# Constants from one step matrix, narrow w_in pieces and an earlier flush in a sliding-window attention and MoE kernel

## The chip, the core and the metric

The kernel runs on one core of one Trainium2 chip. The time is device time in microseconds of one execution of the whole program; six runs of the kernel before gave a median of 321.82 us (321.56 to 323.2). The page and the trace describe one further execution, taken by the hardware profiler.

A core has five engines that run their own instruction streams: TensorE (PE, with its weight loads shown apart as PEld), VectorE (DVE), ScalarE (ACT), GpSimd (POOL) and SyncE (SP). POOL and SP issue DMA transfers, which 16 DMA engines of the core carry out. Each stream is executed in its order; streams wait for one another through semaphores.

## What is computed

```python
# q, k, v: [8 batches, 8 heads, 576 positions, 64], float32
mask = np.abs(pos[:, None] - pos[None, :]) <= 32
scores = where(mask, q @ k.T / sqrt(64), -1e9)
x = softmax(scores) @ v                      # as [4608 tokens, 512]
h = x @ w_in                                 # w_in  [512, 2048]
g = where(h >= 1, h, where(h <= -1, 0, (h + 1) ** 2 / 4))
out = g @ w_out                              # w_out [2048, 512], out [4608, 512] float32
```

A query sees only the keys that lie at most 32 positions away, so the scores are a band.

## The kernel before

**Attention.** Keys are taken in blocks of 64. A block of 64 keys meets the 128 queries from 32 before it to 32 behind it, and the band in that tile of 64 x 128 is the same for every block. Two heads lie side by side in the 128 partitions, so partitions 0 to 63 and 64 to 127 hold the same band. `scores` (L201) multiplies keys with queries, takes the exponential on ACT (L225) and applies the band in one of two ways. In the first 14 slots (`eng = None`, L446) the band is added before the exponential: `add_mask` (L194) multiplies the identity with `bias`, 0 inside the band and -1e30 outside, into PSUM. From slot 14 on DVE multiplies the exponentials by `mask4` or `mask8` (L192), which are 1 and 0. `sums` (L255) multiplies the exponentials with v and with ones, and its `end` takes the reciprocal of the row sums on ACT (Ln, L289, then Exp, L290, called lr and rc) and leaves the product of the two for DVE in the list `muls`. `flush` (L301) issues what is in that list: it writes xT, the attention output with tokens along the free axis.

**The second part.** 4608 tokens are cut into 18 blocks of 256 tokens, 2048 hidden columns into 8 pieces of 256. One piece of one block is a slot `a` of the main loop (L444), with t = a // 8 and f = a % 8. In a slot PE computes hp from xT and columns 256 f to 256 f + 256 of w_in (L466, 8 matmuls), ACT makes rr (L470), DVE makes mx and gT (L472, L473). Then `run` issues the attention work that a table of positions (`at`, L366 to L406) gives to this slot, and `quarter` multiplies gT with a quarter of w_out (L417, 4 matmuls) for an earlier block. So slots 0 to 7 need the tokens 0 to 255 and all of w_in, piece by piece; slot 8 needs the tokens 256 to 511, of which the last come from the sums at slots 3, 4 and 5. `quarters` (L363) puts the eight quarters of block 0 at slots 9 to 15; those that use the last quarter of w_out stand at slot 15. A flush stands before hp in slot 0 and in the slots above 5, and one behind gT in every slot.

**The start.** SP loads q of batch 0 as float32. Everything else goes through POOL's queue, which casts to bfloat16 on the way, in this order: k of batch 0, first half (positions come in two halves); v of batch 0; w_in's columns 0 to 512 in four pieces of 256 columns (two halves of the partitions each); q and k of batch 0, second half; the rest of w_in, the columns 512 to 1024 in pieces of 256 and the columns 1024 to 2048 in pieces of 512; w_out's first quarter (L108); q and k of batch 1, first half; w_out's second and third quarters; v of batch 1; w_out's last quarter; q and k of batch 1, second half; batch 2. Loads on POOL's queue take turns on eight semaphores: each waits until the eighth before it has landed. Between k and v POOL makes the identity (`make_identity`), and between v and w_in the four selects that cut the band into `bias` (L127, L129). DVE makes mask4 and mask8 from `bias` by a compare (L343).

**Before the loop** (L327 to L355) q and k of the first half are transposed by PE (`tpose`, L168; with the identity), copied out of PSUM by ACT and DVE in parts (L181), and the first scores and sums are made; `keep_warm` puts in matmuls on zeros. At slots 1 and 1.5 the second half follows: q's transposes, four warm matmuls, k's transposes. The second part of k's transposes uses the PSUM tile that DVE's copy of q's second part has to leave first.

Of the kernel before, what the change touches and what calls it, by code (L numbers as in the profile page):

```python
# [7 lines left out]

FP = mybir.dt.float32
BF = mybir.dt.bfloat16  # L10
AF = mybir.ActivationFunctionType
ALU = mybir.AluOpType
# [3 lines left out]
def kernel(  # L16
# [19 lines left out]
    nc = tc.nc  # L36
    B, H, S, D = q.shape
    NT, DM, DFF = out.shape[0], 512, 2048
# [4 lines left out]
    TAIL = S - MAIN  # L43
# [4 lines left out]
    const = ctx.enter_context(tc.tile_pool(name="const", bufs=1))  # L48
# [13 lines left out]

    ident = const.tile([128, 128], BF, name="ident")
    ones = const.tile([128, 64], BF, name="ones")
    bias = const.tile([128, 128], BF, name="bias")
    mask4 = const.tile([128, 8 * 128], BF, name="mask4")
    mask8 = const.tile([128, 4 * TAIL], BF, name="mask8")
    w_in = const.tile([128, 4, DFF], BF, name="w_in")
# [5 lines left out]
    V, P, A = nc.vector, nc.gpsimd, nc.scalar  # L74
# [20 lines left out]
    def load_v(b, n):  # L95
        if b not in vn:
            vn[b] = nat.tile([128, 2 * NC, 2, D], BF, name="vn", tag="vn", bufs=3)
        h, a = divmod(n, 2)
        y = NY * h + 2 * a
        nc.gpsimd.dma_start(out=vn[b][64 * a:64 * a + 64, :, h], in_=v[b, y:y + 2].rearrange("y s d -> (y s) d")  # L100
                            .rearrange("(c r) d -> r c d", r=64))
# [9 lines left out]
    early = ctx.enter_context(tc.tile_pool(name="early", bufs=1))  # L111
# [5 lines left out]
    A.preload_act_table_set("natural_log_exp_and_others")  # L117
    warm = const.tile([128, 512], BF, name="warm")
    V.memset(warm, 0.0)
    V.memset(bias, 0.0)  # L120
    make_identity(nc, ident)
    for n in range(4):
        load_v(0, n)

    for h in range(2):
        r = slice(64 * h, 64 * h + 64)
        P.affine_select(out=bias[r], in_=bias[r], compare_op=ALU.is_ge, fill=-1e30, base=0,  # L127
                        channel_multiplier=-1, pattern=[[1, 128]])
        P.affine_select(out=bias[r], in_=bias[r], compare_op=ALU.is_ge, fill=-1e30, base=64,  # L129
                        channel_multiplier=1, pattern=[[-1, 128]])  # L130
    V.memset(ones, 1.0)
    for t in qTs:
        V.memset(t[:, 0:PAD], 0.0)
    def mix(small, large):

        for n in range(0, max(len(small), 2 * len(large)), 2):
            for fn, *x in large[n // 2:n // 2 + 1] + small[n:n + 2]:
                fn(*x)

    def halves(b, half):  # L140
        return [(load_long, b, half, t, y) for t in range(2) for y in range(NY)]

    def put(todo):
        for fn, *x in todo:
            fn(*x)

    w = [(load_w_in, c, c + d, h) for c, d in ((0, 256), (256, 256), (512, 256), (768, 256), (1024, 512), (1536, 512))
         for h in range(2)]
    put(w[:4] + halves(0, 1) + w[4:])
    mix(halves(1, 0), [(load_w_out, 0)])  # L150
    put([(load_w_out, 1), (load_w_out, 2)] + [(load_v, 1, n) for n in range(4)])
# [7 lines left out]
    def qkT(b, t):  # L159
        if t == 0:  # L160
            return qTs[b % 3][:, PAD:]
        if b not in kT:
            kT[b] = ktp.tile([128, NY * S], BF, name="kT")
        return kT[b]

    HD = (slice(0, 64), slice(64, 128))
# [27 lines left out]
    def add_mask(ps, n, w):  # L194
        for a in range(2):
            for h in range(2):
                nc.tensor.matmul(ps[h][HD[a], :n * w].rearrange("p (n j) -> p n j", n=n), ident[HD[h], HD[h]],
                                 bias[HD[h], :w].rearrange("p (n j) -> p n j", n=1).to_broadcast([64, n, w]),
                                 start=True, stop=False, skip_group_check=True)

    def scores(b, ys, pars, cs, eng, pool=ps_s):  # L201
# [99 lines left out]
    def flush():  # L301
        while muls:
            muls.pop(0)()
# [4 lines left out]
    def tp1(pool):  # L308
        if pool is ps_h:
            return pool.tile([128, 8, 128], BF, name="tp", tag="hp")  # L310
        return pool.tile([128, 2, 8, 128], BF, name="tp", tag="bb")[:, 0]

    def keep_warm(n, pool, tag):

        z = pool.tile([128, 512], FP, name="z", tag=tag)
        for _ in range(n):
            nc.tensor.matmul(z, warm[:, :128], warm, start=True, stop=True)

    def cast(x, nm, cut):

        y = early.tile([128, 9, 2, D], BF, name=nm)
        o, i = y.rearrange("p j h d -> p h j d"), x.rearrange("p h (j d) -> p h j d", d=D)
        V.tensor_copy(o[:, :, :cut], i[:, :, :cut])
        A.copy(o[:, :, cut:], i[:, :, cut:])
        return y.rearrange("p j h d -> p j (h d)")

    with tc.tile_pool(name="ps_p", bufs=1, space=bass.MemoryType.PSUM) as ps_p:  # L327
        keep_warm(14, ps_h, "hp")

        V.memset(qkT(0, 0).rearrange("d (y s) -> d y s", y=NY)[:, :, S // 2:352], 0.0)  # L330
        for b in range(LONG):
            V.memset(qkT(b, 0).rearrange("d (y s) -> d y s", y=NY)[:, :, S - PAD:], 0.0)
        V.memset(qkT(0, 1).rearrange("d (y s) -> d y s", y=NY)[:, :, S // 2:320], 0.0)
        qn[0, 0] = cast(q32, "qb", 5)
        qq = [tpose(0, n, 0, (A.copy, V.tensor_copy)[n], tp1(ps_h)) for n in range(2)]
        for x in qq:
            x()
        kk = [tpose(0, n, 1, (A.copy, V.tensor_copy)[n], tp1((ps_n, ps_p)[n])) for n in range(2)]
        keep_warm(3, ps_h, "hp")
        for x in kk:  # L340
            x()
        for m, n, w in ((mask4, 8, 128), (mask8, 4, TAIL)):
            V.tensor_scalar(m.rearrange("p (n j) -> p n j", n=n),  # L343
                            bias[:, 0:w].rearrange("p (n j) -> p n j", n=1).to_broadcast([128, n, w]), -1.0, None,
                            op0=ALU.is_ge)
        scores(0, (0, 1), (0, 2), (0, 2), None)
        scores(0, (0, 2), (0, 1), (2, 3), None, ps_n)
        scores(0, (1, 2), (0, 2), (0, 2), None, ps_p)
        keep_warm(5, ps_h, "hp")
        e0 = sums(0, 0, 0, TB)  # L350
        keep_warm(2, ps_h, "hp")
        e1 = sums(0, 1, 0, TB, ps_p)
        keep_warm(8, ps_h, "hp")
        e0()
        e1()  # L355
# [45 lines left out]
    for b in range(LONG, B):  # L401
        a = sl[5 * (b - 1) - 7] - 17
# [22 lines left out]
    def run(pos):  # L425
        todo = []
        for fn, *x in ev.get(pos, []):
            if fn is sums:
                todo.append(sums(*x))
            elif fn is tpose:  # L430
                part = x.pop()
                todo.append(tpose(*x, (A.copy, V.tensor_copy)[part if pos < 2 or pos > 16 else 0], tp1((ps_s, ps_n)[part])))
                if part:
                    while todo:
                        todo.pop(0)()
            elif fn is keep_warm:
                keep_warm(*x)
            else:
                pool = (x.pop(),) if x[-1] in (ps_s, ps_n, ps_o) else ()
                fn(*x, eng, *pool)  # L440
        for end in todo:
            end()

    for a in range(NF * NB + NF):  # L444
        t, f = divmod(a, NF)
        eng = None if a < 14 else V  # L446
        post = [x for n, x in quarters if n == a] if a < 2 * NF else [a - NF]
        for b, x in loads.get(a, []):
            if x < 2:
                load_nat(b, x)  # L450
            else:
                for n in range(4):
                    load_v(b, n)
        if a == 0 or a > 5:
            flush()
        if t < NB:
            if t not in gT:
                gT[t] = gtp.tile([128, 2 * NF, TB], BF, name="gT", tag="gT")
            r0 = TB * t % RING
            if a in (6, 7):  # L460
                hp = ps_o.tile([128, 2, TB], FP, name="hp", tag="op")
            else:
                hp = ps_h.tile([128, 2, TB], FP, name="hp", tag="hp")
            for j in range(2):
                for n, kk in enumerate((0, 2, 1, 3)):
                    nc.tensor.matmul(hp[:, j], w_in[:, kk, 256 * f + 128 * j:256 * f + 128 * j + 128],  # L466
                                     xT[:, kk, r0:r0 + TB], start=n == 0, stop=n == 3)

            rr = ewp.tile([128, 2, TB], FP, name="rr")
            A.activation(rr, hp, AF.Relu, scale=0.5, bias=0.5)  # L470
            mx = ewp.tile([128, 2, TB], FP, name="mx")
            V.tensor_max(mx, hp, rr)  # L472
            V.scalar_tensor_tensor(gT[t][:, 2 * f:2 * f + 2], rr, 1.0, mx, op0=ALU.min, op1=ALU.mult)  # L473
        flush()
        run(a)
        for x in post:
            quarter(x)
        run(a + 0.5)
        for x in xps.get(a, []):
            xpose(*x)  # L480
# [30 lines left out]
```

## Time and profile before

| | |
|---|---|
| median of 6 runs | 321.82 us |
| profiled execution | 322.24 us |
| its span, first to last instruction | 320.4 us |
| granted PE clock over the span | 0.995 |
| PE busy | 306.4 us (96%) |
| DVE busy | 247.3 us (77%) |
| ACT busy | 193.3 us (60%) |
| POOL busy | 87.5 us (27%) |
| DMA packets, bytes | 121573, 34.52 MB |

The span is a little shorter than the time of the execution, which also holds what lies around the first and the last instruction. Busy PE time is not PE at its peak, since matmuls are pipelined and their ends are modelled.

A row of the page's groups gives line, engine, operation and tiles, how often it ran, the busy time, the mean of one in ns, and the idle time of its engine just before with what ended it:

```profile
L466 PE MATMUL hp<-xT,w_in 128*128 128x256 bf16 x1152 | 150.5, 274 | 4.3 <-DMA w_in<-in_moe_w_in_dram 2.7
L417 PE MATMUL op<-w_out,gT 128*128 128x512 bf16 x576 | 146.6, 380 | 0.0
```

The two matmul groups of the second part hold most of PE's time. POOL's timeline of the start gives start, length, engine, line and tiles; the times of the DMA rows are those in which POOL issues them, not those of the transfers:

```profile
3.53 0.25 POOL masks.py:197 MEMSET ident<- 128x128 bf16 x1
3.86 0.29 POOL masks.py:199 TENSOR_SCALAR_AFFINE_SELECT ident<-ident 128x128 bf16<-128x128 bf16 x1
4.10 3.41 POOL L100 DMA_DIRECT2D vn<-in_v_dram  x4
7.47 0.35 POOL L127 TENSOR_SCALAR_AFFINE_SELECT bias<-bias 64x128 bf16<-64x128 bf16 x1
7.89 0.28 POOL L129 TENSOR_SCALAR_AFFINE_SELECT bias<-bias 64x128 bf16<-64x128 bf16 x1
8.24 0.29 POOL L127 TENSOR_SCALAR_AFFINE_SELECT bias<-bias 64x128 bf16<-64x128 bf16 x1
8.60 0.29 POOL L129 TENSOR_SCALAR_AFFINE_SELECT bias<-bias 64x128 bf16<-64x128 bf16 x1
8.84 2.57 POOL L104 DMA_DIRECT2D w_in<-in_moe_w_in_dram  x4
```

### The profile page before, as it was taken

Reading aid. Unit: us, or ns where it says so; the run is one execution under the profiler, and the core shown is the slowest. Engines: PE = TensorE matmul, PEld = TensorE weight load, DVE = VectorE, ACT = ScalarE, POOL = GpSimd, SP = SyncE. Lnnn points to the kernel's source line nnn. Section 1 sums busy time; section 2 is a strip of 40 time slices with the busy share of each in tenths; the row PEclk is TensorE's granted clock in tenths of the full one; section 3 lists DMA queues with packets and bytes.
Section 4 is the critical chain, followed back from the end, with each engine's and each line's share of the span. In section 5 each row is a group of like instructions: output and inputs, shape, how many; then the busy total and the mean of one; then the engine's idle time right before and its main releaser. Section 6 shows DMA issues by size and latency. Waiting matters only on the chain.

```text
span 320.4 us, 8552 instructions
## 1 busy us (share of the span) xinstructions
PE 306.4 (96%) x3651; PEld 202.0 (63%) x3651; DVE 247.3 (77%) x385; ACT 193.3 (60%) x318; POOL 87.5 (27%) x122
## 2 busy tenths in 40 slices
PE   6977899999999999999999999999999999999995
PEld 3555665666666666666666666666666666666652
DVE  2364966797888888888888888888888888877760
ACT  2756656676776666765666666566566766554421
POOL 8982837798204504121411200000000000000000
PEclk9997999999999999999999999999999999999999
DMA  9999999999999999929991947004420000000111
GB/s 144 149 132 202 142 175 159 173 161 165 152 153 172 167 126 176 166 50 104 191 160 41 108 99 117 35 35 106 88 58 35 33 35 35 34 35 35 46 52 65
DMA packets 121573, 34.52 MB, mean 108 GB/s; under 512 B 108736, under 2 KB 116672, under 8 KB 121536
## 3 DMA queue, kind: packets, MB, share of 16 engines
q0 software_dynamic: 92672, 18.06, 72.2%
q1 hardware_dynamic: 28864, 15.93, 21.3%
q8 instruction: 28, 0.46, 0.6%
q14 instruction: 9, 0.07, 0.1%
HBM read 36.70 MB, written 9.44 MB: 144 GB/s over the span
## 4 chain that ended last, share of the span: by engine, by line
PE 83%; POOL 5%; DVE 3%; ACT 3%; DMA 3%; issue 1%; POOLq 0%; ACTq 0%
PE op L417 38%; PE hp L466 37%; PE bb L283 6%; DMA w_in<-in_moe_w_in_dram 3%; PE bb L217 2%; POOL w_in L104 2%; POOL kn L84 1%; PE tp L178 1%; DVE mx L472 1%; POOL vn L100 1%; ACT rr L470 1%; DVE gT L473 1%; POOL qn L84 1%; DVE xT L295 1%; ACT lr L289 1%
## 5 line engine op out<-in xcount | busy, mean ns | idle before, releaser
L466 PE MATMUL hp<-xT,w_in 128*128 128x256 bf16 x1152 | 150.5, 274 | 4.3 <-DMA w_in<-in_moe_w_in_dram 2.7
L417 PE MATMUL op<-w_out,gT 128*128 128x512 bf16 x576 | 146.6, 380 | 0.0
L466 PEld LDWEIGHTS <-w_in 128*128 128x128 bf16 x1152 | 111.9, 98 | 46.2 <-issue 5.4
L470 ACT ACTIVATE rr<-hp 128x512 f32<-128x512 f32 x144 | 85.7, 595 | 91.7 <-PE hp L466 89.5
L472 DVE TENSOR_TENSOR mx<-hp,rr 128x512 f32<-128x512 f32 x144 | 99.3, 690 | 42.0 <-ACT rr L470 40.0
L473 DVE SCALAR_TENSOR_TENSOR gT<-rr,mx 128x512 bf16<-128x512 f32 x144 | 99.6, 692 | 4.9
L417 PEld LDWEIGHTS <-gT 128*128 128x128 bf16 x576 | 53.4, 98 | 41.6
L225 ACT ACTIVATE pt<-bb 128x1024 bf16<-128x1024 f32 (+1 forms) x33 | 33.2, 1012 | 6.3 <-PE bb L217 5.1
L100 POOL DMA_DIRECT2D vn<-in_v_dram x32 | 27.5, 881 | 30.6 <-PE bb L217 29.2
L295 DVE TENSOR_TENSOR xT<-bb,rc 128x512 bf16<-128x512 f32 (+1 forms) x32 | 21.0, 657 | 9.7 <-ACT rc L290 9.1
L422 ACT COPY osb<-op 128x512 f32<-128x512 f32 x36 | 20.8, 581 | 11.6 <-PE op L417 11.2
L290 ACT ACTIVATE rc<-lr 128x512 f32<-128x512 f32 (+2 forms) x40 | 23.5, 587 | 1.3
L92 POOL DMA_DIRECT2D qn<-in_q_dram x10 | 12.3, 1245 | 40.0 <-DMA qT<-qn 40.0
L289 ACT ACTIVATE lr<-bb 128x512 f32<-128x512 f32 (+2 forms) x40 | 22.1, 552 | 1.1 <-PE bb L283 1.0
L283 PE MATMUL bb<-pt,ones 64*64 64x256 bf16 (+3 forms) x352 | 19.7, 258 | 1.3 <-DVE xT L295 0.6
L192 DVE TENSOR_TENSOR pt<-pt,mask 128x1024 bf16<-128x1024 bf16 (+1 forms) x33 | 20.3, 614 | 0.2 <-ACT pt L225 0.2
L283 PE MATMUL bb<-pt,vn 64*64 64x128 bf16 (+3 forms) x712 | 18.5, 206 | 0.0
L283 PEld LDWEIGHTS <-vn 64*64 64x64 bf16 x712 | 17.0, 109 | 0.0
L283 PEld LDWEIGHTS <-ones 64*64 64x64 bf16 x352 | 10.3, 106 | 10.2 <-issue 9.0
L84 POOL DMA_DIRECT2D kn<-in_k_dram x24 | 13.1, 554 | 10.1 <-DMA w_out<-in_moe_w_out_dram 4.3
L217 PE MATMUL bb<-qT,kT 64*64 64x128 bf16 x520 | 13.0, 217 | 0.8 <-DVE kT L181 0.8
L84 POOL DMA_DIRECT2D qn<-in_q_dram x20 | 11.0, 564 | 7.4 <-DMA w_out<-in_moe_w_out_dram 3.1
(44 smaller groups left out, 100.1 us busy)
## 6 DMA issues: line engine op xcount, KB each, us to landing
out_dram<-osb SPq DMA_DIRECT2D x36, 256.0 KB, 2.3
vn<-in_v_dram POOLq DMA_DIRECT2D x32, 144.0 KB, 5.8
qn<-in_q_dram POOLq DMA_DIRECT2D x10, 288.0 KB, 7.3
kn<-in_k_dram POOLq DMA_DIRECT2D x10, 288.0 KB, 8.8
w_out<-in_moe_w_out_dram POOLq DMA_DIRECT2D x4, 512.0 KB, 10.2
kn<-in_k_dram POOLq DMA_DIRECT2D x24, 72.0 KB, 3.9
qn<-in_q_dram POOLq DMA_DIRECT2D x20, 72.0 KB, 4.9
w_in<-in_moe_w_in_dram POOLq DMA_DIRECT2D x8, 128.0 KB, 4.4
```

The source lines that it names most:

```text
L84: (eng or nc.gpsimd).dma_start(out=dst[b, half][32 * y:32 * y + 32], in_=src[b].rearrange("(h y) s d -> y h (s d)", h=2)[y] .rearrange("h ...
L100: nc.gpsimd.dma_start(out=vn[b][64 * a:64 * a + 64, :, h], in_=v[b, y:y + 2].rearrange("y s d -> (y s) d") .rearrange("(c r) d -> r c d", ...
L225: A.activation(p, ps[:, :, :128 * n].rearrange(like, y=m), AF.Exp, scale=D ** -0.5)
L283: nc.tensor.matmul(bb[HD[h], a, o + c0:o + c1], ones[HD[a]] if c is None else vn[b][HD[a], c, h], p(a, h), start=n == 0, stop=True, skip_g ...
L289: A.activation(lr[:, :, :D0], bb[:, :, D0:2 * D0], AF.Ln)
L290: A.activation(rc[:, :, :D0], lr[:, :, :D0], AF.Exp, scale=-1.0)
L295: muls.append(lambda: V.tensor_mul(o, bb[:, :, :D0], rc[:, :, :D0]))
L417: nc.tensor.matmul(o, gT[tt // 2][:, j, 128 * (tt % 2):128 * (tt % 2) + 128], w_out[:, j], start=not done, stop=len(done) == 2 * NF - 1, s ...
L466: nc.tensor.matmul(hp[:, j], w_in[:, kk, 256 * f + 128 * j:256 * f + 128 * j + 128], xT[:, kk, r0:r0 + TB], start=n == 0, stop=n == 3)
L470: A.activation(rr, hp, AF.Relu, scale=0.5, bias=0.5)
L472: V.tensor_max(mx, hp, rr)
L473: V.scalar_tensor_tensor(gT[t][:, 2 * f:2 * f + 2], rr, 1.0, mx, op0=ALU.min, op1=ALU.mult)
```

## The change

Four edits.

- **One step matrix.** A tile `step` of 128 x 257 is set to zero by DVE, and one select on POOL leaves 0 where the column is at least 65 more than the partition, and -1 elsewhere. DVE takes differences of shifted columns of it: by one column for the identity, by 65 for `band` (128 x 192, 1 inside the band and 0 outside); `bias` is (band - 1) times 2 to the 100th. In `band` and `bias` the partitions 64 to 127 have their band 64 columns further right, so users take the columns from 64 h on. The select stands behind k's loads, before v's; the five other POOL instructions go.
- **Masks.** mask4 and mask8 are no longer made by a compare before the loop, but by four copies of `band` (two for each half of the partitions) in slot 1, behind gT and its flush, ahead of the attention work of that slot.
- **w_in** is loaded in pieces of 256 columns throughout: the columns 1024 to 2048 come in eight loads where there were four. The order of the columns stays.
- **Flush.** The flush before hp also stands in the slots 4 and 5.

```diff
-    V.memset(bias, 0.0)
-    make_identity(nc, ident)
+    step = early.tile([128, 257], BF, name="step")
+    V.memset(step, 0.0)
+    P.affine_select(out=step, in_=step, compare_op=ALU.is_ge, fill=-1.0, base=-65, channel_multiplier=-1,
+                    pattern=[[1, 257]])
     for n in range(4):
         load_v(0, n)
-    for h in range(2):
-        r = slice(64 * h, 64 * h + 64)
-        P.affine_select(out=bias[r], in_=bias[r], compare_op=ALU.is_ge, fill=-1e30, base=0,
-                        channel_multiplier=-1, pattern=[[1, 128]])
-        P.affine_select(out=bias[r], in_=bias[r], compare_op=ALU.is_ge, fill=-1e30, base=64,
-                        channel_multiplier=1, pattern=[[-1, 128]])
     V.memset(ones, 1.0)
     for t in qTs:
         V.memset(t[:, 0:PAD], 0.0)
+    V.tensor_sub(ident, step[:, 65:193], step[:, 64:192])
+    V.tensor_sub(band, step[:, 65:], step[:, :192])
+    V.tensor_scalar(bias, band, 1.0, 2.0 ** 100, op0=ALU.subtract, op1=ALU.mult)
...
-    w = [(load_w_in, c, c + d, h) for c, d in ((0, 256), (256, 256), (512, 256), (768, 256), (1024, 512), (1536, 512))
-         for h in range(2)]
+    w = [(load_w_in, c, c + 256, h) for c in range(0, DFF, 256) for h in range(2)]
...
-                                 bias[HD[h], :w].rearrange("p (n j) -> p n j", n=1).to_broadcast([64, n, w]),
+                                 bias[HD[h], 64 * h:64 * h + w].rearrange("p (n j) -> p n j", n=1)
+                                 .to_broadcast([64, n, w]),
...
-        for m, n, w in ((mask4, 8, 128), (mask8, 4, TAIL)):
-            V.tensor_scalar(m.rearrange("p (n j) -> p n j", n=n),
-                            bias[:, 0:w].rearrange("p (n j) -> p n j", n=1).to_broadcast([128, n, w]), -1.0, None,
-                            op0=ALU.is_ge)
...
-        if a == 0 or a > 5:
+        if a == 0 or a > 3:
             flush()
...
         flush()
+        if a == 1:
+            for h in range(2):
+                for m, n, w in ((mask4, 8, 128), (mask8, 4, TAIL)):
+                    V.tensor_copy(m[HD[h]].rearrange("p (n j) -> p n j", n=n), band[HD[h], 64 * h:64 * h + w]
+                                  .rearrange("p (n j) -> p n j", n=1).to_broadcast([64, n, w]))
         run(a)
```

More of the change, by code (lines that the diff above doesn't have):

```diff
@@ L5 @@
 from concourse import mybir
-from concourse.masks import make_identity
 from concourse._compat import with_exitstack
@@ L64 @@
     ones = const.tile([128, 64], BF, name="ones")
-    bias = const.tile([128, 128], BF, name="bias")
+    band = const.tile([128, 192], BF, name="band")
+    bias = const.tile([128, 192], BF, name="bias")
     mask4 = const.tile([128, 8 * 128], BF, name="mask4")
```

## The prediction

> **What bounds the kernel now.** I read the page's slices first. The rows are TensorE (PE), its granted clock, the share of the DMA engines and what they moved, 8 us to a slice:
>
> ```profile
> PE   6977899999999999999999999999999999999995
> ...
> PEclk9997999999999999999999999999999999999999
> DMA  9999999999999999929991947004420000000111
> GB/s 144 149 132 202 142 175 159 173 161 165 152 153 172 167 126 176 166 50 104 191 160 41 108 99 117 35 35 106 88 58 35 33 35 35 34 35 35 46 52 65
> ```
>
> PE is full from slice 5 on, so nothing behind 35 us can be won except where PE waits there. Every part of the change lies in the first five slices, or acts on the loads of the first seven. Next the chain of waits for the start (start, length, what):
>
> ```profile
> 18.94 8.17 DMA w_in<-in_moe_w_in_dram
> 27.11 0.14 issue
> 27.24 1.40 PE hp L466 x8
> ```
>
> The slot loop at a=4 waits for the first w_in piece of 512 columns. Then PE's timeline, with its idle time and the releaser in brackets:
>
> ```profile
> 19.78 0.47 PE L178 MATMUL tp<-ident,kn 128*64 128x128 bf16 x10 [1.01 <-DMA kn<-in_k_dram]
> 20.40 0.41 PE L178 MATMUL tp<-ident,kn 128*64 128x128 bf16 x8 [0.15 <-DVE qT L181]
> ...
> 27.24 1.40 PE L466 MATMUL hp<-xT,w_in 128*128 128x256 bf16 x8 [2.26 <-DMA w_in<-in_moe_w_in_dram]
> ...
> 34.48 1.91 PE L466 MATMUL hp<-xT,w_in 128*128 128x256 bf16 x16 [0.83 <-DVE xT L298]
> ...
> 53.28 0.81 PE L466 MATMUL hp<-xT,w_in 128*128 128x256 bf16 x6 [0.53 <-DVE xT L295]
> ```
>
> Between 34.48 and 53.28 PE has no gap. Last, the windows of the load phase (PE, PEld, DVE, ACT, POOL busy, clock, DMA share, GB/s):
>
> ```profile
> 19.00:22.00 3.00, 1.61 (x25) 1.30 (x26) 2.04 (x3) 0.75 (x1) 3.00 (x6) 1.00 1.13 139
> 22.00:24.00 2.00, 2.00 (x47) 1.35 (x49) 0.99 (x2) 1.66 (x3) 1.21 (x3) 1.00 1.04 132
> 24.00:30.00 6.00, 3.74 (x88) 2.75 (x88) 2.46 (x4) 3.73 (x8) 1.61 (x4) 0.81 1.22 200
> ```
>
> The DMA engines hold work throughout (share about 1 or more). 19 to 22 is 256-column pieces (128 KB over 256 rows, 512 B each), 24 to 30 is 512-column pieces (1 KB rows): 139 against 200 GB/s.
>
> **Part 1, constants (L119 to L133).** Removed on POOL: the identity's memset and select (0.25 + 0.29, with gaps 3.53 to 4.10) and four bias selects (7.51 to 8.89, 1.4 us). Added: one select over 257 columns after the kn loads. 128 columns took 0.29, so 0.29 to 0.6; it ends at about 4.1, where the first vn load started before. So the vn loads keep their time and w_in's first issue moves from 8.84 to about 7.45. That lead mostly turns into queueing: vn's last load lands at 6.63 + 4.2 = 10.9, in the same queue, and the first w_in lands at 12.0 already. DVE gets three small operations (0.2 to 0.3 us each, by the 128x384 compare at 0.28) that wait for the select. Behind them stand five memsets (0.46) and the cast of q at 6.22, which waits for q. 4.1 + 0.8 + 0.5 = 5.4, so 0.8 us of cover; if the select took 1.4 us, every later start would slip. Bias no longer waits on POOL, but L197 at 9.08 also stood behind the three warm matmuls that end there: 0.
>
> **Part 2, masks in slot 1.** The two compares leave 9.01 to 9.62, where DVE then idles 3.84: 0. Two pairs of copies of the same sizes (0.405 and 0.282, 0.61 a pair as overlapped) come after slot 1's gT, which ends at 19.72: 1.15 us in front of the qT copy at 19.64. Behind that copy PE waits (20.40 above), then the kT copy and slot 2. Without the kn wait of 1.01 (kn is issued 1.4 earlier), PE does the first ten kn transposes at 18.8, then idles from about 19.2 to 21.5. Slot 2's hp starts at 21.8 instead of 21.27: this part alone costs 0.5 there.
>
> **Part 3, narrow w_in.** Slot 4 needs only columns 1024 to 1280. POOL issues twelve pieces in the second batch, where eight stood. Landings before (issue plus time to landing): 20.3, 21.1, 21.9, 22.7 for four narrow pieces, 25.8, 27.1, 28.4, 29.7 for four wide ones, w_out's first quarter at 20.74 + 11.6 = 32.3. With 20.0 for the first and 0.9 each, the pairs land at 20.9, 22.7, 24.5, 26.3, 28.1, 29.9. PE, going on from 21.8 with warm durations (hp 0.98 a slot, scores 0.7, 0.46 and sums 0.55), comes to slot 4 at 25.5, slot 5 at 27.0, slot 6 at 28.4, and slot 7 at 29.4: only slot 7 waits, 0.5, and that is covered by the next part.
>
> **Part 4, flush at slots 4 and 5.** The product of slot 3's sums now stands before slot 4's mx. It needs rc, which is in ACT's order ahead of rr, so it runs while ACT makes rr (0.60): 0. Slot 4's product, at 33.35 before because gT of slot 5 was ahead, goes into the DVE idle time ahead of mx. ACT and DVE in their new order (lr 0.55, rc 0.58, rr 0.60; products 0.6, mx and gT 0.69) finish the last product of the first half at 31.65, where it was 34.43. So slot 8 starts at 31.7, not 34.48: **2.8 us earlier** with a warm PE.
>
> The clock takes some of it. After the 2.26 us gap the slice has clock 7, and the 8 matmuls at 29.49 take 1.85 for 1.04. [...] The trace shows half clock after 2.26, from 27.8 to 31.2. The new gap at 19.2 is as long, so by the row hp and scores of slots 2 and 3 run slow: about 1.0 us, and slot 8 at 32.7, 1.8 earlier. Either value stands; the next part makes it matter little.
>
> **Part 5, what is late next: the loads.** Each load waits for the landing of the eighth before it, and the DMA queue is full until 50. w_out's last quarter is issued at 38.00 and lands after 11.6, at 49.6; slot 15's quarter needs it at 50.44. Slack 0.8, and 0.53 more since PE idles before 53.28 anyway: 1.3 us. (qn, kn and the other w_out quarters have 3 us.) The load chain is rigid: the last kn of this group (32.62) waits for w_out's first quarter, the other w_out loads stand behind it, and from there the queue is full. So a shift d of that landing (32.3) moves the landing at 49.6 by d, and the kernel gains at most 1.3 - d.
>
> d from both sides. By landings, 0.79 a piece: 20.0 + 11 x 0.79 + 2.6 = 31.3, d = -1.0. By the rate, 131 KB at 139 GB/s = 0.94: 32.9, d = +0.6; and if the stall between 22.7 and 25.8 (3.1 where a wide piece then takes 1.3) comes again where rows grow at w_out, d = +2.5. [...] I take 0.9, nearer the rate because POOL keeps issuing: 20.0 + 9.9 + 2.6 = 32.5, d = **+0.2**.
>
> **Sum.** Start: -1.8 to -2.8. Given back waiting for w_out at slot 15: 0.7 to 1.7. Net -(1.3 - 0.2) = **-1.1 us**. The profiled execution took 322.24 (span 320.4 and 1.8 around it), so 321.1; on the median of the runs, 321.82, that is **320.7**. A difference under 0.3%, 0.97 us, is about what a measurement here can't tell from none.
>
> **Rivals.**
> - *The loads keep up* (d below -0.5): the start's 1.8 to 2.8 stays, 319.0 to 320.0, say 319.4. For it: landings 0.79 apart, and the 1.4 us lead. Against: the rate. Chance 0.16.
> - *Half clock at slot 15.* PE's wait there is 1 to 2 us; if it halves the clock for 3.4 us, 1.7 us of PE work is lost where PE is the bound: 320.7 + 1.7 = 322.4, no change. For it: the gap at 24.98. Against: 18.8 to 21.3, with 1.6 us of idle in pieces, kept clock 1.00. Chance 0.20.
> - *Slower: narrow rows hold up the loads.* Place: w_out's last quarter in slot 15. From d = 1.3 on it lands too late even for the old schedule. At d = 2 it costs 0.7, and since PE then idles over 2 us in one piece there, half clock adds 1.7: 324.2. For it: 512 B rows at 139 GB/s, 12 x 128 KB of them. Against: it needs the stall again, or 1.02 us a piece. Chance 0.22.
>
> **Numbers.** Forecast (gain 0.5 to 1.9) 0.42; the rivals as given. Faster by over 0.3%: 0.16 and 0.26 of the forecast's 0.42, 0.42. Within: the other 0.16 and 0.15 of half clock, 0.31. Slower: 0.22 and 0.05 of half clock, 0.27. The likeliest's own range is 319.9 to 321.3; for 8 in 10 it reaches to the first rival's 319.4 and well into the slower one, 323.3.
>
> **What would show it.** Right: no PE wait for w_in at slot 4; a wait of 1 to 2.4 us for DVE's qT copy near 21; slot 8 at 31.7 to 32.7; narrow pieces landing 0.8 to 1.0 apart; PE waiting for w_out before the quarters of slot 15 near 49.8. Wrong: no wait there (the loads keep up), the wait in w_in's slots 5 to 7, q's cast later than 6.2, or mask copies much over 1.2 us in sum.

## The result and the profile after

The change makes no difference that this measurement can tell: 321.67 us as the median of 28 runs (320.14 to 323.15) against 321.75 for the kernel before (63 runs), a ratio of 0.9992 with a 95% interval of 0.998 to 1.0003. The forecast was -1.1 us; measured are -0.3 by the ratio and -0.1 by the medians.

The profiled execution after took 322.82 us (span 320.7), so it is one of the long ones; why is seen below. Its slices, in the rows shown of before:

```profile
PE   7969899999999999999999999999999999999995
...
PEclk9987999999999999999999999999999999999999
DMA  9999999999999999929991946005320000000111
GB/s 148 166 141 192 137 177 163 179 159 168 150 148 164 159 118 177 163 53 103 191 164 39 108 96 119 35 35 107 85 60 35 33 35 35 36 33 35 46 52 65
```

The third slice (16 to 24 us) has lost PE time (6 for 7) and clock (8 for 9). The fourth has won PE time (9 for 7), and its clock is 7 as before. PE's timeline tells what happened there:

```profile
18.61 0.47 PE L178 MATMUL tp<-ident,kn 128*64 128x128 bf16 x10
21.84 0.64 PE L178 MATMUL tp<-ident,kn 128*64 128x128 bf16 x8 [2.75 <-DVE qT L181]
22.41 1.89 PE L463 MATMUL hp<-xT,w_in 128*128 128x256 bf16 x8
...
28.58 1.05 PE L463 MATMUL hp<-xT,w_in 128*128 128x256 bf16 x8
...
34.73 1.91 PE L463 MATMUL hp<-xT,w_in 128*128 128x256 bf16 x16 [1.31 <-DVE xT L299]
...
50.69 1.90 PE L414 MATMUL op<-w_out,gT 128*128 128x512 bf16 x8
...
53.53 0.82 PE L463 MATMUL hp<-xT,w_in 128*128 128x256 bf16 x6 [0.52 <-DVE xT L296]
```

The wait for w_in ahead of slot 4 (2.26 us) is gone. In its place stands a wait of 2.75 us at k's second transposes in slot 1, for DVE's copy of q. DVE, at that time:

```profile
19.54 1.49 DVE L475 COPY mask<-band 64x1024 bf16<-64x1024 bf16 x4
21.07 0.72 DVE L181 COPY qT<-tp 128x512 bf16<-128x512 bf16 x1
```

The four mask copies hold it up. Then hp of slot 2 takes 1.89 us where slot 4's takes 1.05. The windows (PE, PEld, DVE, ACT, POOL busy, clock, DMA share, GB/s) name the reason:

```profile
21.50:24.90 3.40, 3.06 (x32) 1.86 (x35) 1.00 (x2) 0.57 (x1) 3.13 (x6) 0.50 1.30 160
24.90:28.30 3.40, 3.40 (x72) 2.26 (x68) 1.54 (x3) 2.09 (x6) 1.34 (x3) 0.56 1.33 184
28.30:31.50 3.20, 3.20 (x101) 2.47 (x89) 2.33 (x4) 3.14 (x6) 1.59 (x3) 1.00 1.23 202
```

PE runs at half clock for 6.8 us, from 21.1 to 27.9. So slot 8 starts at 34.73, where it started at 34.48: in this execution the start has won nothing.

**Every run carries its granted clock**, and that sorts the times. A stretch of 3.41 us at half clock, the length of the one in the trace before (27.77 to 31.18), lowers the mean over 320 us by 0.0053, two by 0.0106; the runs lie near 0.999, 0.994 and 0.989. For the kernel before, the table takes the runs that were made beside the experiments, in three sets; one of 325.32 us is left out as slow, which leaves 157:

| granted clock | before: runs, median us | after: runs, median us |
|---|---|---|
| 0.997 and above | 73, 321.31 | 7, 320.46 |
| 0.992 to 0.996 | 79, 322.23 | 17, 321.70 |
| 0.991 and below | 5, 323.46 | 4, 322.96 |
| all | 157, 321.79 | 28, 321.67 |

Within each class the changed kernel is 0.5 to 0.9 us faster. (These are runs of different sets: the median of before at full clock is 321.2, 321.3 and 321.7 in its three, so the differences are good to about half a microsecond.) But it falls to the lower classes in 21 of 28 runs, the kernel before in 84 of 157. That eats much of the gain: with before's shares of the classes, the three differences would make about 0.7 us, an estimate from the table.

**Another part is lost outside the span.** The time less the span from first to last instruction is 1.73 to 1.85 us in all runs of before beside the experiments, and 2.07 to 2.20 in all 28 of the changed kernel: 0.3 us that no engine's timeline shows. The experiments below tell which edit brings it.

### The profile page after: what moved, and what is told of

It reads as the page before. It is cut to its first block, busy times and chain, and to the rows that moved or that the text cites. A ratio compares the mean times of both kernels' runs of the same rounds, so it can differ in the third digit from the quotient of the medians.

```text
span 320.7 us, 8557 instructions
## 1 busy us (share of the span) xinstructions
PE 307.5 (96%) x3651; PEld 202.6 (63%) x3651; DVE 249.4 (78%) x390; ACT 193.2 (60%) x318; POOL 88.6 (28%) x121
## 4 chain that ended last, share of the span: by engine, by line
PE 85%; DVE 6%; ACT 5%; DMA 1%; issue 1%; SPq 0%; ACTq 0%; DVEq 0%
PE op L414 38%; PE hp L463 37%; PE bb L284 5%; PE bb L218 2%; DVE mx L469 2%; PE tp L178 2%; ACT pt L226 1%; DVE gT L470 1%; ACT rc L291 1%; DMA q<-in_q_dram 1%; ACT lr L290 1%; DVE xT L296 1%; ACT rr L467 1%; PE bb L197 1%; DVE mask L475 0%
## 5 line engine op out<-in xcount | busy, mean ns | idle before, releaser
L92 POOL DMA_DIRECT2D qn<-in_q_dram x10 | 12.3, 1243 | 41.2 <-DMA qT<-qn 41.2
L84 POOL DMA_DIRECT2D kn<-in_k_dram x24 | 13.0, 548 | 8.8 <-DMA w_out<-in_moe_w_out_dram 4.1
L92 POOL DMA_DIRECT2D kn<-in_k_dram x10 | 12.2, 1228 | 2.1 <-DMA kn<-in_k_dram 1.8
```

The source lines that it names most:

```text
L92: nc.gpsimd.dma_start(out=x[:, :, h], in_=src[b, NY * h:NY * h + NY].rearrange("y s d -> (y s) d") .rearrange("(u p) d -> p u d", p=128))
```

## The experiments

Theory A: the mask copies in slot 1 stop PE, its clock halves, and this eats what the loads win. Theory B: the loads cap the gain at slot 15. Each kernel's median stands beside its ratio to the runs of before made with it, with the 95% interval, and then its runs with clock 0.997 and above, called full clock.

**Mask copies in slot 13.**

```diff
-        if a == 1:
+        if a == 13:
```

> The changed kernel with the four mask copies moved from slot 1 to slot 13, nothing else. Theory A (the copies in slot 1 hold up DVE's copy of q, PE idles 2.75 us and its clock halves for 6.8 us, which eats what the loads and the flush win): PE's gap before k's second transposes falls from 2.75 to about 1.2 us, the clock stays full, slot 8 starts at 31.5 to 32.0 instead of 34.7, and the time is 2.0 to 2.8 us below the kernel before, 319.0 to 319.8. Theory B (the loads, w_out's last quarter above all, cap the gain at slot 15): the start is won but given back there in a wait of 1.5 us or more, and the time is within 1 us of the changed kernel's 321.7.

320.51 us, 0.9969 (0.995 to 0.9987); 18 of 22 runs at full clock, their median 320.37. PE's timeline:

```profile
20.21 0.41 PE L178 MATMUL tp<-ident,kn 128*64 128x128 bf16 x8 [1.23 <-DVE qT L181]
...
31.11 1.91 PE L463 MATMUL hp<-xT,w_in 128*128 128x256 bf16 x16 [0.81 <-DVE xT L299]
...
48.51 1.89 PE L414 MATMUL op<-w_out,gT 128*128 128x512 bf16 x8 [1.37 <-DMA w_out<-in_moe_w_out_dram]
```

The gap is 1.23 and slot 8 starts at 31.11, 3.4 us ahead of before, as theory A wants. Then PE waits 1.37 us at slot 15 for w_out, as theory B wants. The profiled execution (319.70) is at the fast end; the median is 1.2 us below before, between the times that the two theories gave. Both mechanisms are at work, one behind the other.

**A filler in PE's gap, copies left in slot 1.**

```diff
-    at(1.5, *through(0, 1, 1))
+    k0, k1 = through(0, 1, 1)
+    at(1.5, k0, (keep_warm, 8, ps_o, "op"), k1)
```

> The changed kernel with eight matmuls on zeros (about 1.7 us) between the two parts of k's transposes in slot 1, where PE idles; the copies stay. If the half clock is the larger part of theory A's loss: the clock stays full from 19 to 28, slot 8 starts at 32.0 to 32.7, time 1.3 to 2.3 us below before, 319.5 to 320.5. If the delay of DVE's copy by itself is the loss: slot 8 not before 34, time 321.2 to 322. Theory B: a wait at slot 15, 321 or more.

320.43 us, 0.9968 (0.9954 to 0.9983); all 19 runs at full clock.

```profile
21.21 0.41 PE L178 MATMUL tp<-ident,kn 128*64 128x128 bf16 x8 [0.48 <-DVE qT L181]
...
32.08 1.91 PE L464 MATMUL hp<-xT,w_in 128*128 128x256 bf16 x16 [1.31 <-DVE xT L299]
...
49.77 1.89 PE L415 MATMUL op<-w_out,gT 128*128 128x512 bf16 x8 [1.58 <-DMA w_out<-in_moe_w_out_dram]
```

The copies still delay the transposes to 21.21, yet the time is that of the version without them. So of the harm in slot 1 the clock is all that can be seen at the end; the delay by itself disappears in the wait at slot 15. This is the clearest test: eight matmuls that compute nothing keep the clock full in 19 of 19 runs, where it was so in 7 of 28, and win 1.2 us by the medians, 0.8 by the ratios.

**No wait for w_out at slot 15** (masks in slot 13; block 0's last quarters use the third quarter of w_out).

```diff
-            nc.tensor.matmul(o, ..., w_out[:, j],
+            nc.tensor.matmul(o, ..., w_out[:, j - 4 if ff == 3 and tt < 2 else j],
```

> The version with the masks in slot 13, with block 0's last quarters in slot 15 multiplied with the third quarter of w_out instead of the last (so they don't wait for its landing; those 256 rows of the output are not the reference's). If that landing is the cap of the gain: no wait ahead of slot 15's quarters, slot 16 0.8 to 1.4 us earlier (half a us of it may return as the wait for xT there), median 0.5 to 1.2 below 320.5, 319.3 to 320.0. If it is no cap: 320.5 as before.

319.58 us, 0.9932 (0.9906 to 0.9958), six runs, five at full clock with 319.36.

```profile
47.25 1.90 PE L414 MATMUL op<-w_out,gT 128*128 128x512 bf16 x8
49.19 0.38 PE L464 MATMUL hp<-xT,w_in 128*128 128x256 bf16 x2
50.10 0.82 PE L464 MATMUL hp<-xT,w_in 128*128 128x256 bf16 x6 [0.53 <-DVE xT L296]
```

The wait is gone, the one for xT behind it (0.53) is back, and the full-clock median is 1.0 us below that of the version with the wait. So the landing does cap the gain. By how much is less certain: the intervals of the two ratios overlap (0.995 to 0.9958), the runs are of different sets, and the two profiled spans differ by 0.4 us only (317.6 and 317.2).

The cap is seen from another side in the seven traces that show a wait there. Behind slot 15 the timelines, read to 70 us, have no wait of PE over 0.64 us, and those of before and after none longer to the end, so the end follows that start at a fixed distance, whatever the start of the kernel won:

| kernel | wait for w_out | slot 15's quarters start | span less that start |
|---|---|---|---|
| masks in slot 13 | 1.37 | 48.51 | 269.1 |
| masks in slot 13, no early flush, filler | 1.29 | 48.97 | 269.1 |
| masks in slot 13, no early flush (second) | 1.74 | 49.43 | 269.1 |
| filler, copies in slot 1 | 1.58 | 49.77 | 269.1 |
| masks in slot 13, wide w_in | 1.57 | 50.04 | 269.1 |
| constants alone | 1.65 | 50.20 | 269.1 |
| masks in slot 1 alone | 0.84 | 50.95 | 269.0 |

In these executions the landing of w_out's last quarter sets the time. In the six traces without such a wait, and without fillers in its place, the distance is 269.9 to 270.0: without the wait at slot 15, PE loses time at the wait for xT behind it. So of a wait at slot 15, 0.9 us comes back.

**Narrow w_in alone** (before, with the change's w_in line).

> The kernel before with w_in in 256-column pieces throughout, nothing else. Theory A: slot 4 no longer waits for w_in at 27.2, PE comes to it at about 25, the half clock from 27.8 goes, slot 8 starts at 32 to 33 (the late flush still holds it up), time 1.0 to 2.0 below before, 319.8 to 320.8. Theory B (narrow rows delay the loads behind them): w_out's last quarter lands at 50 or later and the time is that of before or up to 1 us above, 321.7 to 322.8.

321.25 us, 0.9985 (0.9963 to 1.0008), no difference told. Half clock in 7 of 14 runs, the profiled one among them, as in 32 of the 64 runs of before made with them:

```profile
22.07 1.86 PE L465 MATMUL hp<-xT,w_in 128*128 128x256 bf16 x8 [1.25 <-DMA w_in<-in_moe_w_in_dram]
...
31.43 0.28 PE L282 MATMUL bb<-pt,ones 64*64 64x192 bf16 x4 [1.76 <-DVE xT L294]
```

Slot 4's wait is gone; waits at slots 2 and 5 stand instead, and slow matmuls follow each (the hp behind the first takes 1.86 where slot 3's takes 1.05, the 32 behind the second 5.33 for the 3.81 of other traces; the granted clock of the run is 0.989), so theory A's gain of 1 to 2 us does not come. w_out's last quarter, issued at 38.26, took 11.4 and landed at 49.7, as before (49.6). The part of theory B that narrow rows delay the loads behind them falls.

**Wide w_in, the rest of the change with masks in slot 13.**

> The changed kernel with the mask copies in slot 13 and w_in's columns 1024 to 2048 in 512-column pieces as before. Theory A: the constants move POOL's issue 1.4 us ahead, but the DMA queue is full, so slot 4 still waits for w_in, until about 26.5; half clock in part of the runs; the flush wins about 0.6: time 0.5 to 1.2 below before, 320.5 to 321.2, so the narrow pieces are worth 1 to 2 us in e1. Theory B: as fast as e1 or faster, since no narrow rows stand ahead of w_out.

321.36 us, 0.9987 (0.9968 to 1.0005). 9 of 22 runs at full clock, their median 320.53, near the narrow version's 320.37. In its trace slot 4 waits 1.67 us for w_in. What the narrow pieces buy here is fewer half clocks: 18 of 22 runs at full clock with them. Alone, on the old schedule, they bought none (7 of 14 above).

**Constants alone**, masks copied in the old place.

> The kernel before with the constants from one step matrix alone; the masks are copied from the band in the old place before the loop, w_in and the flush as before. The lead of POOL, 1.4 us, mostly turns into queueing: w_in's first wide pieces land at 26 to 27, slot 4 starts 0.3 to 0.8 us earlier than 27.24, and the time is 0.2 to 1.0 us below before, 320.7 to 321.5. If the lead carries through in full: slot 4 at 25.7, 320.2 or less. If it is all queueing: 321.7.

321.47 us, 0.9996 (0.9976 to 1.0015), no difference told, 4 of 14 runs at full clock.

```profile
26.50 1.03 PE L468 MATMUL hp<-xT,w_in 128*128 128x256 bf16 x8 [1.61 <-DMA w_in<-in_moe_w_in_dram]
...
50.20 1.89 PE L419 MATMUL op<-w_out,gT 128*128 128x512 bf16 x8 [1.65 <-DMA w_out<-in_moe_w_out_dram]
```

Slot 4 starts 0.7 us earlier (26.50 for 27.24), and slot 15, at 50.20 for 50.44, takes most of it back.

**Masks in slot 1 alone** (before; the two compares made there, twice).

> The kernel before with the two mask compares moved from before the loop into slot 1, behind gT, and made twice there (so that the sum is about that of the four copies); nothing else. Theory A: PE's gap before k's second transposes is about 1.6 us there (k itself lands late), the clock halves from about 21 in most executions, slots 2 and 3 run slow, and slot 4 starts at 27.3 to 28.5; slower by 0.3 to 1.5 us, 322.0 to 323.2. Theory B or a hidden delay: slot 4 waits for w_in until 27.1 in any case, no change, 321.4 to 322.0.

321.82 us, 1.0004 (0.9987 to 1.002): on the old schedule they cost nothing that can be told, and theory A's loss did not come. 15 of 22 runs lost clock, 37 of 67 of before made with them. The profiled one did not, and waited for w_in ahead of slot 4 until 28.05 (2.06 us) and for w_out at slot 15 (0.84).

**The flush**, from two sides. First, the changed kernel without it in slots 4 and 5:

```diff
-        if a == 0 or a > 3:
+        if a == 0 or a > 5:
```

> The changed kernel without the flush ahead of hp in slots 4 and 5; the mask copies stay in slot 1. If the flush is worth the 0.6 us or more that the prediction gave it: slot 8 later, time 322.0 to 322.5. If it only changes the order on a chain of ACT and DVE that is as long either way: 321.3 to 321.9, as the changed kernel.

321.95 us, 1.0001 (0.9985 to 1.0017); the changed kernel has 0.9992, no difference that can be told. Then the same with the masks in slot 13:

> The changed kernel with the mask copies in slot 13 and without the flush ahead of hp in slots 4 and 5. If the flush matters in the start: slot 8 waits for the product of slot 5's sums 0.6 to 1.4 us longer than in the version with it (31.1), so 31.7 to 32.5. But w_out's last quarter at slot 15 caps the gain (a wait of 1.37 us there with the flush), so by theory B that wait shrinks by as much and the time stays that of the version with the flush, 320.2 to 320.8. If there is no cap: 320.9 to 321.6.

320.05 us, 0.9951 (0.9935 to 0.9968), and a second time:

> The version with the masks in slot 13 and without the early flush a second time, on the chip of this call: 319.8 to 320.5, 0.4 to 0.65% below before, by theory A.

320.32 us, 0.9952 (0.9935 to 0.9968), six runs.

```profile
29.34 0.28 PE L284 MATMUL bb<-pt,ones 64*64 64x192 bf16 x4 [1.75 <-DVE xT L296]
29.75 3.81 PE L463 MATMUL hp<-xT,w_in 128*128 128x256 bf16 x32
...
49.43 1.89 PE L414 MATMUL op<-w_out,gT 128*128 128x512 bf16 x8 [1.74 <-DMA w_out<-in_moe_w_out_dram]
```

Without the early flush PE waits at slot 5's sums for slot 3's product, and passes slots 6 to 9 in one go; with it PE waits at slot 8. Slot 8 is at 31.65 here (two slots of 0.95 behind 29.75), at 31.11 with the flush. That half microsecond does not reach the end. In the first trace of this kernel (320.43, granted clock 0.995) the matmuls are slow from 29.2 on, the 32 of slots 6 to 9 take 5.21 us for 3.81, and there is no wait at slot 15; its span is 318.7, that of the second (clock 0.999) 318.5. So 0.2 us of the half clock is seen between the two spans: the second loses nearly as much at its wait for w_out.

The version with the late masks and no early flush has the lowest median of those with all the reference's work, 0.5% below before. Its interval overlaps that of the version with the flush. But the time outside the span decides for it: 2.06 us or more in every one of the 119 runs of the six kernels with the early flush, 1.85 us or less in every one of the 264 runs of the seven without it, and two pairs of them differ in that edit alone. So the early flush costs 0.3 us that the timelines don't show. It lies behind the last instruction: the clock record goes on for 2.38 us there in the trace after, for 2.05 in that of before. Why is open. Less that part, the medians of the versions with and without it are 318.4 and 318.3 with the masks in slot 13, and 319.5 and 320.2 with the masks in slot 1: there the flush seems to shorten the span, and gives half of it back.

**Fillers against the rest of the half clock.** Masks in slot 13, five matmuls between k's transposes, six behind slot 15's sums:

> The changed kernel with the mask copies in slot 13, five matmuls on zeros between the two parts of k's transposes, and six behind the sums of slot 15, where PE waits for w_out's last quarter. If half clock in part of the executions makes the spread of 319.7 to 322.7 in the version without fillers: a full clock in the trace, the median falls to 319.7 to 320.2 and few runs lie above 321. If the spread has another cause: median 320.5 with the same spread, or higher by up to 1 us since the fillers stand in PE's way.

320.62 us, 0.9964 (0.9945 to 0.9983): full clock in 22 of 22 runs, yet the same spread (319.28 to 322.35) and no lower median: a miss. A spread is left that is not the clock's. The table's starts of slot 15 differ by 2.4 us between kernels, so the landing of w_out is the nearest candidate. It does vary between executions of one kernel: the two traces of the version without the early flush have it at 48.7 and 49.4. Whether it makes the whole spread is not shown. With the filler in slot 1 alone and no early flush:

> Masks in slot 13, no early flush, and five matmuls on zeros between the two parts of k's transposes. If the idle 1.2 us there still halves the clock in part of the executions: median below the version without the filler (320.05), 319.4 to 319.9, and few runs above 321. If not: 320.0 to 320.5.

320.47 us, 0.9955 (0.9936 to 0.9973), six runs, three of them with half clock. A miss: a filler in slot 1 does not cover the later wait for xT at slot 5 (1.89 in its trace, which kept its clock). That this wait is what halved the clock in the three runs is not shown; in the first trace without the filler, the slow matmuls (5.21 us for 3.81) do follow the idle time there (0.85 and 0.84 us).

## Why the prediction was right or wrong

The time lies in the wide range, 319.4 to 323.3, but not in the forecast's own, 319.9 to 321.3. The mechanisms named were at work, but the forecast case was not the one that came: a gain of 1.1 us was forecast, 0.3 measured. The result is that of the half-clock rival (no change, 0.20), which was right on the mechanism and wrong on the place: slot 1, not slot 15.

- **Part 1** held. The first vn load was issued at 3.98, the first w_in at 7.35 and landed at 12.2: the lead became queueing. The cast of q started at 5.93.
- **Part 2** was too small. The copies took 1.49 us for the 1.15 taken, the transposes ahead of the gap ended as forecast, and the gap was 2.75 for 2.3.
- **Part 4 held the step that failed**: "by the row hp and scores of slots 2 and 3 run slow: about 1.0 us, and slot 8 at 32.7", with "the next part makes it matter little". The term was mis-sized twice. In the profiled execution the half clock lasted two stretches of 3.41 us, where before's trace had shown one: from slot 2's hp to slot 4's PE took 6.2 us (22.41 to 28.58) for the warm 3.7 (21.8 to 25.5), so the clock cost 2.5 us, not 1.0, and slot 8 came at 34.73. And it was one number for all runs, though it differs from run to run: 7 of 28 had no half clock, 17 one stretch, 4 two. Those 7 have 320.46, 0.85 below before's at full clock, nearly the forecast. The others are 1.2 us longer and more. That slot 1's gap does this, the filler shows; where the stretch of the 17 lies, no trace shows.
- **A term was put at nothing.** The sum took over the 1.8 us around the span. They became 2.1, so 0.3 us of the missing 0.8 was lost there, with the early flush.
- The sum was also made against one execution of before that itself had a half-clock stretch (clock 0.995), when 73 of 157 runs have none. Removing that stretch was counted as a gain for every run; for those 73 there was none to remove.
- The early flush was part of the forecast 2.8 us at the start. With the masks in slot 13 nothing of it is left at the end, and it costs the 0.3 us outside the span.
- **Part 3 and 5.** The narrow pieces landed from 15.39 + 3.7 = 19.1 to 22.59 + 6.6 = 29.2, 0.92 apart: the 0.9 taken was right. w_out's first quarter landed at 23.30 + 8.6 = 31.9, d = -0.4 for +0.2, since the first piece came 0.9 earlier than assumed. Its last landed at 37.56 + 10.7 = 48.3, 1.3 earlier, so the chain behind is not rigid. The slower rival did not come (by its own sum its d of 1.3 needs 1.00 us a piece, not 1.02); that the loads keep up came true for the profiled execution, which had no wait at slot 15. The cap itself was right: with the clock kept and the copies in slot 1, the filler's version gains 1.2 us for the forecast 1.1. That the two numbers are so close is in part luck. In its trace the landing was close to the forecast (49.7 for 49.8), but 0.9 us came back behind slot 15 where 0.53 was taken, and the 0.3 us outside the span were left out.

## What to carry to other kernels

Work that has no hurry (masks that are first used thirteen slots later) is not free because its engine has room on the average: look at what is queued behind it and who waits there. If the waiting engine is PE, look at the granted clock behind the gap, not at the gap alone (here 6.8 us at half clock behind 2.75); a few matmuls on zeros in it can be worth as much as removing the delay (here eight: 320.43 us, and 320.51 with the copies moved). Sort the runs by granted clock before comparing medians: a change can win in each class and lose it again by moving runs between classes. And compare the time outside the span too: a change can lose there what no timeline shows.

## What the runs showed that was not expected

- **In the traces of before and after, half clock came in whole stretches of 3.41 us.** It was granted from 27.77 to 31.18 us before (one) and from 21.09 to 27.91 after (two); from the first clock record (3.87 and 4.02) to that fall it was seven and five of them at full clock. PE's busy time in some of these stretches, by the modelled ends of the matmuls, and the clock:

| kernel | stretch | PE busy, us of 3.41 | clock in it | clock in the next |
|---|---|---|---|---|
| before | 17.53 to 20.94 | 2.13 | 1.00 | 1.00 |
| before | 24.35 to 27.76 | 1.15 | 1.00 | 0.50 |
| before | 27.76 to 31.17 | 3.41 | 0.50 | 1.00 |
| changed | 17.68 to 21.09 | 1.40 | 1.00 | 0.50 |
| changed | 21.09 to 24.50 | 2.67 | 0.50 | 0.50 |
| changed | 24.50 to 27.91 | 3.41 | 0.50 | 1.00 |
| changed | 31.33 to 34.74 | 2.10 | 1.00 | 1.00 |

- **Gaps of nearly one length did not all cost clock.** Behind the 2.26 us ahead of slot 4 before, the next two hp took 1.40 and 1.85 us; behind the 2.06 us at the same place with the masks in slot 1 alone they took 1.03 and 1.05, and the granted clock of that run is 1.00. Between executions of one kernel it differs too: 84 of 157 runs of before lost clock, and 21 of 28 of the changed kernel. What decides it, no run shows.
- Half clock did not last equally long: after, a second stretch followed the one with 2.67 us of busy PE; in narrow w_in alone it came to 3.4 us in all (clock 0.78 from 20 to 23 us and 0.74 from 23 to 27), with PE idle until 22.07 and busy from there to 27.
- 512 B rows moved at 139 GB/s between 19 and 22 us before (POOL busy 3.00 of 3.00 us) and at 170 between 22 and 26 us after (3.50 of 4.00); the 1 KB rows of before moved at 200. While the last narrow pieces landed (24.9 to 28.3, after; 766 packets of 512 B and 213 of 1 KB) it was 184, so in these traces the length of the rows alone did not set the rate.
